# Fused chunk attention and Fourier mixing: how the first group's tables, weights and weight sums are spread over the engines

## The chip, the cores and the metric

The kernel runs on one core of a Trainium2 chip. A time is the device time of one execution in microseconds (us). A version is compared by the median of several executions; one further execution was recorded by the hardware profiler, and everything that is read from a trace is about that one. Instructions are issued by TensorE (PE), VectorE (DVE), ScalarE (ACT), GpSimd (POOL) and SyncE (SP). Each runs its own list in the order in which the program gives it. DMAs are issued from SP, ACT or POOL and wait in that engine's list until what they need is there.

## The reference

Two blocks follow each other. Shapes: batch 8, 8 heads, 576 tokens, head size 64, so 512 features; the MLP is 2048 wide.

```
# attention inside chunks of 64 tokens, per batch and head
scores = q_c @ k_c.T / 8                        # 64 x 64
attn   = exp(scores - max); attn /= sum(attn) + 1e-9
x      = attn @ v_c                             # heads side by side: (8, 576, 512)
# Fourier mixing and MLP
u   = x + real(fft(fft(x, over tokens), over features))
un  = (u - mean(u)) / sqrt(var(u) + 1e-6)       # over features
out = u + relu(un @ w_ch1) @ w_ch2              # 512x2048, 2048x512
```

The weights arrive as 64-bit floats and are turned into 32-bit ones on the chip; everything else is 32-bit. The Fourier transforms are products with tables of cosines and sines.

## The kernel before, in words

**Tiles and groups.** A tile is 128 tokens. Tiles 0 to 4 belong to batch 0: a "rest" tile (the middle chunk of batches 0 and 1), then LO(1), HI(1), LO(0), HI(0), pairs from the front and from the back of the sequence, which the transform folds onto each other (`fold`). Four tiles are a group for the MLP, group g being batch g's four tiles; the rests make a group at the end.

**Batch 0** is alone on the chip. `attention_early` (L507) runs the five tiles in a software pipeline: `att_T` transposes q and k on PE and copies them with ACT, `att_S` makes the scores, `softmax` uses DVE and ACT, `att_P` transposes back, `att_V` multiplies with v and normalizes on DVE. `shift_early` (L439) then moves single rows between tiles, since the fold needs token 0 apart; `fold` (L467) makes sums and differences. `fourier_early` (L686) multiplies them with the token table `tk` (L704 to L708), with the feature tables `cos_d`, `sin_d` (L734), adds the result to x, normalizes (`normed`, L770) and transposes (`turned`, L787) for the MLP. `keep_warm(n)` (L1098) gives PE n matmuls without a purpose of their own (each is two records in the trace).

**Tables.** `load_tables` (L221) loads the token table into `start` by eight DMAs and two rows into `first_rest` by two more. `turn_tables` (L245) copies it into `tk`, each run of 64 columns reversed, by four copies of 128x384 and two small ones.

**Weights.** `pieces` (L263) lists 32 pieces of 128x512, sixteen of each weight. `load_weight(i)` (L276) brings a piece into one of seven staging spaces; pieces from number 8 on have five of them, pieces from 26 on three. `round_weight(i)` (L284) starts piece i (two DVE and three ACT instructions: L295 to L299) and ends piece i-1 (three DVE instructions: L304 to L306), frees that piece's space and issues the next load. `round_next()` calls it for the next piece.

**The main loop** (L1144 to L1178) counts steps t. In a step `mlp(g)` gives PE one slice of the MLP: for group 0 steps 1 to 16 are the first product (four matmuls on one piece of the first weight), steps 17 to 32 the second one. Then `side(b)`, the next batch's attention and Fourier part, advances by as many steps as are due: batch 1 is spread over t = 3 to 25, batch 2 begins at t = 26. Its step 21 (at t = 22) and step 22 (t = 23) are the two halves of the token product L607, which ACT copies out of PSUM (L632 to L642); steps 23 to 25 (t = 24, 25, 25) are the feature products (L659) with additions and statistics. Then the step rounds weight pieces: none if the side step was a "heavy" one (a fold), else one, or two when t <= 4, t % 4 == 0 or t >= 18.

**Sums of the second weight.** From group 1 on the MLP uses a block scheme with seven products in place of eight, which needs sums of weight quarters. `keep2(i)`, i = 0 to 3 (L843), makes four sums of 128x512 (L854, POOL) and then stores seven parts to DRAM (L858); each sum and the store is a step of the generator `conv2`. The loop takes two of its steps per t, from t = 20 on (first five steps while the last pieces are rounded, then freely). `keep1` (L826) does the same for the first weight from t = 32 on.

**Normalization.** For group 1, and for the first tile of group 0, `normed` computes `shift = -mean * rstd` on DVE (L781) and lets ACT scale (L782).

**Order of the loads.** SP's list begins with q and k of tiles 0 to 4 (L205; k of tile 0 is on ACT), then weight 0 (L282), v of tiles 3 and 4 (L215, eight DMAs), the feature tables (L237, L238) and weights 1 to 6. POOL's list begins with v of tiles 0 to 2 and the ten DMAs of `load_tables`.

Of the kernel before, what the change touches and what calls it, by code (L numbers as in the profile page):

```python
# [10 lines left out]
ACTF = mybir.ActivationFunctionType  # L11
ALU = mybir.AluOpType
# [4 lines left out]
def kernel(  # L17
# [32 lines left out]
    nc = tc.nc  # L50
    B, H, S, D = q.shape
    DM = H * D
    DFF = w_ch1.shape[1]
    CH = 64
    NC = S // CH
    NM = 2
# [4 lines left out]
    KF = DFF // 128  # L61
    HM, HQ = DM // 2, DM // 4
    NQ = S // 2 + 1
    NS = (NQ + 3) // 4
    NL = 128 * NM
# [3 lines left out]
    scale = 1.0 / float(D) ** 0.5  # L69
# [44 lines left out]
    LO, HI, RE = "lo", "hi", "rest"  # L114
# [10 lines left out]
    at = {t: n for n, t in enumerate(tiles)}  # L125
# [15 lines left out]
    N_LATE, N_EARLY, N_LAST = 5, 8, 26  # L141
# [68 lines left out]
    def load_v(n):  # L210
        t = more_v[n - 3] if 3 <= n < first[1] else v_ring[n % 3]
        for i, (b, c) in enumerate(chunks(n)):
            for e in range(2):
                eng = nc.scalar if n == 0 and e else nc.gpsimd if n < 3 else nc.sync
                eng.dma_start(  # L215
                    out=t[e * CH:(e + 1) * CH, i, :, 0:D],
                    in_=v[b, e:H:2, c * CH:(c + 1) * CH, :].rearrange("j p d -> p j d"),
                )
        vs[n] = t

    def load_tables():  # L221

        t = start[:, 0:(NM + 1) * 2 * NQ].rearrange("p (i r f) -> p i r f", i=NM + 1, r=2)
        for c in range(2 * NM):
            (i, r0), (j, p0) = divmod(c * CH, 128), divmod((NC - 1 - c) * CH, 128)
            nc.gpsimd.dma_start(out=t[r0:r0 + CH, i], in_=seq_tab[p0:p0 + CH, j])
        for r0 in (0, CH):  # L230
            nc.gpsimd.dma_start(out=t[r0:r0 + 1, NM], in_=seq_tab[0:1, 0])
            nc.gpsimd.dma_start(out=t[r0 + 1:r0 + CH, NM], in_=seq_tab[1:CH, NM])
        for i in range(2):
            nc.gpsimd.dma_start(out=first_rest[32 + 32 * i:33 + 32 * i, 0:DM], in_=dim_tab[0:1, 1 + 2 * i, :])

    def load_dim_tables():
        nc.sync.dma_start(out=cos_d, in_=dim_tab[:, 0, :])  # L237
# [7 lines left out]
    def turn_tables():  # L245
        t = start[:, 0:(NM + 1) * 2 * NQ]
        a, b = tk.rearrange("p i r f -> p (i r) f"), t.rearrange("p (i f) -> p i f", f=NQ)
        for c in range(2 * NM):
            nc.gpsimd.tensor_copy(a[:, :, c * CH:(c + 1) * CH], b[:, :, (c + 1) * CH:c * CH:-1])
        nc.gpsimd.tensor_copy(a[:, :, NL:NL + 1], b[:, :, 0:1])  # L250
        nc.gpsimd.tensor_copy(a[:, :, NL + 1:NQ], b[:, :, NL + 1:NQ])

    def turn_dim_tables():

# [184 lines left out]
    def shift_early(i):  # L439

        lows = [xt(at[LO, 0, j])[:, 0:DM] for j in range(NM)]
        rest, kept = xt(rests[0])[0:1, 0:DM], first_rest[0:1, 0:DM]
        if i == 0:
            nc.gpsimd.tensor_copy(kept, lows[1][0:1])
            nc.gpsimd.tensor_copy(lows[1][0:1], lows[1][CH:CH + 1])
            nc.gpsimd.tensor_copy(lows[1][CH:CH + 1], rest)
        elif i == 1:
            nc.gpsimd.tensor_copy(rest, lows[0][0:1])
        else:
            nc.scalar.copy(lows[0][0:1], lows[0][CH:CH + 1])  # L450
            nc.scalar.copy(lows[0][CH:CH + 1], kept)

# [54 lines left out]
    def attention_early():  # L507

        lo, hi = first[0], first[1] - 1

        def ready(n):
            if n == at[LO, 0, 1]:
                shift_early(0)
            if n == at[HI, 0, 1]:
                fold(0, 1)
            if n == at[LO, 0, 0]:
                shift_early(1)
                fold(0, NM)
            if n == at[HI, 0, 0]:
                fold(0, 0)  # L520
            if n + 3 > hi:
                load_v(n + 3)

        att_T(lo)
        att_S(lo)
        for n in range(lo, hi + 1):
            if n < hi:
                att_T(n + 1)
            softmax(n)
            if n > lo:  # L530
                att_V(n - 1)
                ready(n - 1)
            if n == lo + 1:
                turn_tables()
            if n < hi:
                att_S(n + 1)
            if n in (lo, hi):
                keep_warm(1)
            att_P(n)
        shift_early(2)  # L540
        round_next()
        keep_warm(1)
        att_V(hi)
        ready(hi)
        round_next()

    def attention(b):
# [222 lines left out]
    def normed(g, s):  # L770
        if s >= len(groups[g]):
            return
        n = groups[g][s]
        if (g, s) == (0, 3):
            un = one_p.tile([128, NJ, 128], FP32, tag="pT", name="un").rearrange("p j t -> p (j t)")
        else:
            un = three_p.tile([128, DM], FP32, tag="o", name="un")
        mean, rstd = sts.pop(n)
        if g == 1 or (g, s) == (0, 0):
            shift_ = sm_p.tile([128, 1], FP32, tag="shift", name="shift")  # L780
            nc.vector.tensor_scalar(shift_, mean, rstd, -1.0, ALU.mult, ALU.mult)  # L781
            nc.scalar.activation(out=un, in_=natural(n), func=ACTF.Identity, scale=rstd, bias=shift_)  # L782
        else:
            nc.vector.tensor_scalar(un, natural(n), mean, rstd, ALU.subtract, ALU.mult)  # L784
        uns[g, s] = un
# [57 lines left out]
    def keep2(i):  # L843

        m = 2 * i
        b11, b12 = w2[:, m:m + 2, 0:HM], w2[:, m:m + 2, HM:DM]
        b21, b22 = w2[:, HF + m:HF + m + 2, 0:HM], w2[:, HF + m:HF + m + 2, HM:DM]
        to = xall[:, 2 * G:2 * G + 4, 0:DM] if i % 2 else yall
        o1, o2, o3, o4 = (to[:, j].rearrange("p (m e) -> p m e", m=2) for j in range(4))
        for out_, in0, in1, op in (  # L850
            (o1, b12, b11, ALU.subtract), (o2, b22, o1, ALU.subtract),
            (o3, b22, b12, ALU.subtract), (o4, b21, o2, ALU.subtract),
        ):
            nc.gpsimd.tensor_tensor(out=out_, in0=in0, in1=in1, op=op)  # L854
            yield
        to = s2.rearrange("o p (m e) -> o p m e", m=HF)
        for o, a in enumerate((b11, o2, o1, o3, b21, b22, o4)):
            nc.sync.dma_start(out=to[o, :, m:m + 2], in_=a)  # L858
        yield
# [13 lines left out]
    lo, hi = slice(0, 256), slice(256, 512)  # L873
# [199 lines left out]
    with tc.manual_schedule():  # L1073
# [9 lines left out]
        for n in range(first[1]):  # L1083
            load(n)
            if n < 3:
                load_v(n)
        load_tables()
        load_weight(0)
        load_v(3)
        load_v(4)  # L1090
        load_dim_tables()
        for i in range(1, len(spaces)):
            load_weight(i)
        n_w = 0
# [3 lines left out]
        def keep_warm(times):  # L1098

            for _ in range(times):  # L1100
                nc.tensor.matmul(out=idle[:, 0:NQ], lhsT=warm[:, 0:128], rhs=warm[:, 0:NQ], start=True, stop=True)

        def round_next():
            nonlocal n_w
            if n_w <= len(pieces):
                round_weight(n_w)
                n_w += 1
# [33 lines left out]
        n_conv = 0  # L1141
        conv2, conv1 = chain(conv2), chain(conv1)
        t = 0
        for g in range(NG):  # L1144
            for _ in mlp(g):
                t += 1
                heavy = False
                if cur < len(sides):
                    t0 = 2 if cur == 0 else ready_at[cur - 1]
                    t1 = ready_at[cur]  # L1150
                    due = min(sizes[cur], (t - t0) * sizes[cur] // (t1 - t0))
                    while done < due:
                        heavy = next(sides[cur], None) or heavy
                        done += 1
                    if t >= t1:
                        for _ in sides[cur]:
                            pass
                        cur, done = cur + 1, 0
                if not heavy:
                    round_next()  # L1160
                    if t <= 4 or t % 4 == 0 or t >= 18:
                        round_next()
                for _ in range(2):
                    if n_w > N_LAST + 2 and n_conv < 5 or n_w > len(pieces):
                        n_conv += 1
                        next(conv2, None)
                if t == begin[1] - 1:
                    for _ in conv2:
                        pass
                if begin[1] <= t < begin[1] + KF // 2:  # L1170
                    for _ in range(3):
                        next(conv1, None)
                if t == begin[1] + KF // 2:
                    for _ in range(NS2):
                        fetch(2)
                if t == begin[1] + KF:
                    for _ in range(NS1):
                        fetch(1)  # L1178
# [49 lines left out]
```

## Time and profile before

| what | us |
|---|---|
| median of 4 executions | 1126.31 |
| lowest and highest of them | 1124.85, 1128.12 |
| the profiled execution's own time | 1127.69 |
| its span on the core, first to last instruction | 1125.9 |
| PE busy in the span | 1092.0 |
| DVE, ACT, POOL busy | 570.3, 294.5, 309.0 |
| PE's first matmul of the MLP (L889) | starts at 50.99 |

The page of a profile has the busy time of every engine, the span in 40 slices with the clock that PE was granted, the DMA queues, the chain of work that ended last, and the costliest groups of instructions. A line of the timeline has a start and a duration in us, the engine, the line of the kernel, the operation, what it writes and reads, the shape, how many instructions are merged, and in brackets how long the engine was idle before it and what ended that. "PE z L607 <- ACT zr L635" says that PE's instruction of line 607, writing z, waited for ACT's of line 635. The view of stretches gives the busy time of each engine in a stretch, then PE's granted clock (1.00 is full), the busy share of the DMA engines and GB/s.

### The profile page before, as it was taken

The numbers are of one execution on the slowest core, as the hardware profiler recorded it, in microseconds if no ns is written. First come the engines' busy times: TensorE is split into PE (matmuls) and PEld (weight loads), VectorE is DVE, ScalarE is ACT, GpSimd is POOL, SyncE is SP. The second block draws the span as 40 slices with busy tenths as digits, with TensorE's granted clock in tenths as the row PEclk, the third lists the DMA queues.
The fourth block names the chain that finished last, engine by engine and source line by source line (L and its number), as shares of the span: only waits on it lengthen the run. The fifth ranks groups of instructions, "written<-read, shape, count | busy, mean of one in ns | idle before, by whom it ended". The sixth has DMA issues, their size and how long they took to land. (4 is left out here: it accounts for less than half of the span.)

```text
span 1125.9 us, 18754 instructions
## 1 busy us (share of the span) xinstructions
PE 1092.0 (97%) x7036; PEld 846.1 (75%) x7036; DVE 570.3 (51%) x1194; ACT 294.5 (26%) x710; POOL 309.0 (27%) x436
## 2 busy tenths in 40 slices
PE   7999989999999999999999999899999999999998
PEld 5644445446887888778888888788888888888887
DVE  4899975332555355563545355645455434423521
ACT  4688443221112311222122211222132102201210
POOL 6300137326403340053105130154015400130140
PEclk9999989999999999999999999999999999999999
DMA  9767555678475636872567356753654346546332
GB/s 192 224 179 187 153 194 164 182 246 277 163 218 154 177 120 208 235 202 85 173 197 201 125 171 196 218 159 116 203 194 118 113 139 204 141 146 197 91 113 75
DMA packets 147915, 192.73 MB, mean 171 GB/s; under 512 B 66261, under 2 KB 104153, under 8 KB 140657
## 3 DMA queue, kind: packets, MB, share of 16 engines
q1 hardware_dynamic: 145296, 189.57, 56.1%
q0 software_dynamic: 928, 1.57, 0.6%
q8 instruction: 56, 0.92, 0.3%
q10 hardware_dynamic: 1600, 0.39, 0.2%
q14 instruction: 35, 0.28, 0.1%
HBM read 167.22 MB, written 24.12 MB: 170 GB/s over the span
## 5 line engine op out<-in xcount | busy, mean ns | idle before, releaser
L879 POOL TENSOR_TENSOR h<-h 128x256 f32<-128x256 f32 x64 | 55.4, 871 | 414.0 <-PE pb L973 303.3
L1020 PE MATMUL pa<-wb,h 128*128 128x256 f32 x512 | 116.1, 381 | 0.0
L1020 PE MATMUL pb<-wb,h 128*128 128x256 f32 x512 | 115.0, 381 | 0.0
L973 PE MATMUL pb<-unT,wa 128*128 128x256 f32 x448 | 106.6, 381 | 4.3 <-DVE wa L982 4.3
L973 PE MATMUL pb<-wa 128*128 128x256 f32 x448 | 107.3, 382 | 1.4 <-DMA wa<-s 1.4
L973 PE MATMUL pa<-unT,wa 128*128 128x256 f32 x448 | 107.8, 383 | 0.0
L1020 PEld LDWEIGHTS pa<-wb,h 128*128 128x128 f32 x512 | 95.8, 190 | 14.6 <-issue 1.6
L1020 PEld LDWEIGHTS pb<-wb,h 128*128 128x128 f32 x512 | 95.8, 190 | 12.9
L973 PEld LDWEIGHTS pb<-unT,wa 128*128 128x128 f32 x448 | 84.3, 190 | 18.5 <-DVE wa L982 7.0
L973 PEld LDWEIGHTS pb<-wa 128*128 128x128 f32 x448 | 83.4, 190 | 14.7 <-DVE wa L980 1.9
L973 PEld LDWEIGHTS pa<-unT,wa 128*128 128x128 f32 x448 | 83.2, 190 | 11.6
L988 ACT ACTIVATE h<-pa 128x256 f32<-128x256 f32 x56 | 21.5, 384 | 176.4 <-PE pa L973 143.2
L889 PE MATMUL up<-unT,wa 128*128 128x512 f32 x128 | 58.0, 599 | 2.4 <-ACT h L897 1.6
L980 DVE TENSOR_TENSOR wa<-pa,wa 128x256 f32<-128x256 f32 x56 | 23.8, 425 | 70.3 <-PE pa L973 70.3
L927 PE MATMUL dn<-wb,h 128*128 128x512 f32 x128 | 57.7, 599 | 1.4 <-ACT h L897 1.4
L1020 PE MATMUL pa<-wb,yall 128*128 128x256 f32 x256 | 58.2, 382 | 0.0
L973 PE MATMUL pa<-wa 128*128 128x256 f32 x224 | 54.0, 384 | 3.8 <-ACT wa L978 3.8
L906 PE MATMUL up<-unT,wa 128*128 128x512 f32 x128 | 57.5, 598 | 0.0
L1020 PE MATMUL pb<-wb,yall 128*128 128x256 f32 x256 | 57.1, 380 | 0.0
L1020 PE MATMUL pb<-wb 128*128 128x256 f32 x256 | 56.6, 379 | 0.0
L1020 PEld LDWEIGHTS pb<-wb 128*128 128x128 f32 x256 | 48.2, 190 | 6.3
L1020 PEld LDWEIGHTS pa<-wb,yall 128*128 128x128 f32 x256 | 47.7, 190 | 6.9 <-issue 0.5
(235 smaller groups left out, 1676.6 us busy)
## 6 DMA issues: line engine op xcount, KB each, us to landing
wb<-s SPq DMA_DIRECT2D x56, 1024.0 KB
wa<-s SPq DMA_DIRECT2D x196, 256.0 KB
xall<-in_moe_w_ch_dram SPq DMA_DIRECT2D x22, 512.0 KB
q<-in_q_dram SPq DMA_DIRECT2D x96, 112.0 KB
k<-in_k_dram SPq DMA_DIRECT2D x96, 112.0 KB
v<-in_v_dram SPq DMA_DIRECT2D x124, 64.0 KB
yall<-in_moe_w_ch_dram SPq DMA_DIRECT2D x10, 512.0 KB
s<-wb SPq DMA_DIRECT2D x20, 256.0 KB
```

Of the source, the lines that this page charges most:

```text
L879: nc.gpsimd.tensor_tensor(out=h1[:, m, hi], in0=h1[:, m, lo], in1=h1[:, m, hi], op=ALU.subtract)
L889: nc.tensor.matmul(out=up, lhsT=w1[:, kk, m * 128:(m + 1) * 128], rhs=unT[:, kk], start=(kk == 0), stop=(kk == KD - 1),)
L906: nc.tensor.matmul(out=up, lhsT=w1[:, kk, m * 128:(m + 1) * 128], rhs=unT[:, kk], start=(kk == 0), stop=(kk == KD - 1),)
L927: nc.tensor.matmul(out=dn, lhsT=h1[:, m, s * 128:(s + 1) * 128], rhs=w2[:, m, :], start=(m == 0), stop=(m == KF - 1),)
L973: nc.tensor.matmul(out=dst, lhsT=w[:, kk, r], rhs=rhs[o][:, kk], start=(o in (0, 2) and kk == 0), stop=(kk == 1), skip_group_check=True,)
L980: nc.vector.tensor_tensor(out=b, in0=dst, in1=a, op=ALU.add)
L988: nc.scalar.activation(out=h1[:, m, lo], in_=dst, func=ACTF.Relu)
L1020: nc.tensor.matmul(out=dst, lhsT=lhs[:, m], rhs=w[:, m], start=(o in (0, 2) and m == 0), stop=(m == HF - 1), skip_group_check=True,)
```

## The change

The ten DMAs of `load_tables` are issued by SP, no longer by POOL, and come behind q, k and v of all five tiles; weight 0 comes behind them. `turn_tables` runs on ACT, no longer on POOL, and is called at the end of `attention_early`, behind the last tile's fold and three `keep_warm` matmuls; before, it was called in the loop's second round. The row copy of `shift_early(1)` moves from POOL to ACT and is joined with the two ACT copies of `shift_early(2)`; fold(0, NM) follows it. The two `round_next()` of `attention_early` come after all that. In the main loop the rule for a second `round_next()` is written otherwise; the second weight's sums begin only when all pieces are rounded and t >= 23, three generator steps per t, and run on DVE. The shift of group 1's normalization is made by two ACT instructions.

```diff
@@ load_tables: all ten DMAs
-            nc.gpsimd.dma_start(out=t[r0:r0 + CH, i], in_=seq_tab[p0:p0 + CH, j])
+            nc.sync.dma_start(out=t[r0:r0 + CH, i], in_=seq_tab[p0:p0 + CH, j])
...
@@ turn_tables
-            nc.gpsimd.tensor_copy(a[:, :, c * CH:(c + 1) * CH], b[:, :, (c + 1) * CH:c * CH:-1])
-        nc.gpsimd.tensor_copy(a[:, :, NL:NL + 1], b[:, :, 0:1])
-        nc.gpsimd.tensor_copy(a[:, :, NL + 1:NQ], b[:, :, NL + 1:NQ])
+            nc.scalar.copy(a[:, :, c * CH:(c + 1) * CH], b[:, :, (c + 1) * CH:c * CH:-1])
+        nc.scalar.copy(a[:, :, NL:NL + 1], b[:, :, 0:1])
+        nc.scalar.copy(a[:, :, NL + 1:NQ], b[:, :, NL + 1:NQ])
@@ shift_early
-        elif i == 1:
-            nc.gpsimd.tensor_copy(rest, lows[0][0:1])
         else:
+            nc.scalar.copy(rest, lows[0][0:1])
             nc.scalar.copy(lows[0][0:1], lows[0][CH:CH + 1])
             nc.scalar.copy(lows[0][CH:CH + 1], kept)
@@ attention_early
-            if n == at[LO, 0, 0]:
-                shift_early(1)
-                fold(0, NM)
...
-            if n == lo + 1:
-                turn_tables()
...
-        shift_early(2)
-        round_next()
+        shift_early(1)
+        fold(0, NM)
         keep_warm(1)
         att_V(hi)
         ready(hi)
+        keep_warm(3)
+        turn_tables()
+        round_next()
         round_next()
@@ normed
-            nc.vector.tensor_scalar(shift_, mean, rstd, -1.0, ALU.mult, ALU.mult)
+            if g == 0:
+                nc.vector.tensor_scalar(shift_, mean, rstd, -1.0, ALU.mult, ALU.mult)
+            else:
+                nc.scalar.activation(out=shift_, in_=mean, func=ACTF.Copy, scale=-1.0)
+                nc.scalar.activation(out=shift_, in_=shift_, func=ACTF.Identity, scale=rstd)
@@ keep2
-            nc.gpsimd.tensor_tensor(out=out_, in0=in0, in1=in1, op=op)
+            nc.vector.tensor_tensor(out=out_, in0=in0, in1=in1, op=op)
@@ order of the loads
+        load_v(3)
+        load_v(4)
         load_tables()
         load_weight(0)
-        load_v(3)
-        load_v(4)
         load_dim_tables()
@@ main loop
-                    if t <= 4 or t % 4 == 0 or t >= 18:
+                    if t <= 4 or t < KF and t % 4 == 0 or t >= KF + 3:
                         round_next()
-                for _ in range(2):
-                    if n_w > N_LAST + 2 and n_conv < 5 or n_w > len(pieces):
-                        n_conv += 1
+
+                if n_w > len(pieces) and t >= KF + 7:
+                    for _ in range(3):
                         next(conv2, None)
```

## The prediction

> **What bounds the kernel now.** I read the page first.
>
> ```profile
> PE 1092.0 (97%) x7036; PEld 846.1 (75%) x7036; DVE 570.3 (51%) x1194; ACT 294.5 (26%) x710; POOL 309.0 (27%) x436
> PEclk9999989999999999999999999999999999999999
> ```
>
> PE is busy for 97% of the span, and no part of the change removes a matmul from it. So only PE's waits can be won or lost, about 34 us in all, and time in which it runs below full clock: one slice has an 8. Second view, PE's waits in order of size:
>
> ```profile
> PE z L607 <- ACT zr L635: 5.1, 1, 5.1
> ...
> PE pt L316 <- DMA start<-in_k_dram: 1.7, 1, 1.7
> ...
> PE z L704 <- DVE pm L496: 1.0, 1, 1.0
> ```
>
> These three lie where the change works: the first in the second product of group 0, the others in batch 0's lone start. Third view, PE's timeline around the largest:
>
> ```profile
> 144.28 0.76 PE L607 MATMUL z<-tk,pm_rest 64*128 64x289 f32 x4
> 144.97 3.70 PE L927 MATMUL dn<-wb,h 128*128 128x512 f32 x8
> 153.72 4.22 PE L607 MATMUL z<-tk,pm 128*128 128x289 f32 x8 [5.06 <-ACT zr L635]
> 157.88 1.33 PE L607 MATMUL z<-tk,pm_rest 64*128 64x289 f32 x4
> ```
>
> The first half of L607 is done at 145.0. The second needs the PSUM tiles that ACT must copy out, and starts 5.06 us late. Then its matmuls take 4.22 and 1.33 us, where the first half's same ones took 2.11 (at 142.24) and 0.76: the stretch 153 to 155 has a granted clock of 0.50. The wait costs 5.06, the slow clock 2.11 + 0.57 = 2.7. Shorter waits (1.7 at 17.6, 1.6 at 66.5) drew no such stretch.
>
> Why ACT came late, on ACT's and DVE's timelines:
>
> ```profile
> 152.50 0.72 ACT L299 ACTIVATE power<-power,top 128x512 uint32<-128x512 uint32 x1
> 153.13 0.35 ACT L632 COPY zf<-z 128x256 f32<-128x256 f32 x1
> ```
>
> ```profile
> 139.65 1.50 DVE L297 TENSOR_SCALAR power<-xall 128x512 uint32<-128x512 uint32 x1
> 141.07 1.75 DVE L304 SCALAR_TENSOR_TENSOR wb<-xall,wb 128x512 f32<-128x512 uint32 x1
> 142.75 1.75 DVE L305 SCALAR_TENSOR_TENSOR power<-xall,power 128x512 uint32<-128x512 uint32 x1
> ```
>
> ```profile
> 139.31 1.55 POOL L854 TENSOR_TENSOR yall<-wb,yall 128x512 f32<-128x512 f32 x1 [7.83 <-DVE wb L306]
> 140.83 1.45 POOL L854 TENSOR_TENSOR yall<-wb 128x512 f32<-128x512 f32 x1
> 142.24 1.72 POOL L854 TENSOR_TENSOR yall<-wb,yall 128x512 f32<-128x512 f32 x1
> ```
>
> The copy stands in ACT's list behind the rounding of piece 30, and that waits for DVE, which runs pieces back to back at 2.6 us each from 133.9 on. While POOL makes the second weight's sums, DVE's instructions take 1.50, 1.75 and 1.75 where their usual rows say 0.42, 0.69 and 0.69, and the sum L480 at 130.25 (beside POOL's first L854) takes 1.77 instead of 0.69: 1.08 + 1.08 + 1.06 + 1.06 = 4.3 us of DVE lag, handed on to ACT and to PE.
>
> **Part 1, sums off POOL until t = 23.** Counting the loop by hand, all pieces are rounded at t = 22 before and after (the heavy steps are 16 and 18, so the two rules for a second rounding pick the same steps; that edit does nothing). No sum then runs beside the rounding, and the 4.3 us go. Next late is the weight load: pieces from 26 on share three spaces, and from a freed space (end of L305, 144.50, 147.10) to the first use of the piece loaded there (148.01, 150.76) the rows show 3.5 and 3.7 us, while DVE at full speed is back after 0.6 + 2.6 = 3.2 or 3.3. That gives 0.2 to 0.4 of waiting on each of some three pieces, of which I take 0.7 in all. PE's wait falls from 5.06 to 5.06 - 4.28 + 0.7 = 1.5, in the size that kept the full clock. **Gain 3.6 + 2.7 = 6.3.** If the clock falls all the same, only 3.6.
>
> **Part 2, sums on DVE.** Sixteen sums; the nearest row is L306 (two SBUF inputs, 128x512, 0.69, one every 0.61): 9.8 us of DVE, in counts 3, 2, 3, 2, 2, 3, 1 for t = 23 to 29. DVE has gaps there, 4.82 before 165.66 and 2.23 before 170.43, which hide those of t = 23 and 24. The three of t = 25 stand behind the last statistics (178.7) and ahead of batch 2's first softmax, which DVE now starts at 178.62 without a gap. So 3 x 0.61 = 1.8 later come that softmax, ACT's exponent behind it (180.04) and, next in ACT's list, group 1's first normalized tile.
>
> ```profile
> 180.58 0.80 ACT L782 ACTIVATE un<-xall,shift,rstd 128x512 f32<-128x512 f32 x1
> ```
>
> PE transposes that tile at 181.95, a slack of 0.6. The shift on ACT adds two instructions in front (a chained pair of that size, L596 and L597, takes 0.5) and takes off DVE one of 0.2 that nothing waited for. PE so waits 1.8 + 0.5 - 0.6 = 1.7; with DVE's usual slip I take 1.85. The sums of t = 26 to 29 delay transposes and a softmax whose consumers come 5 us later or more (PE's P at 199.5 follows a softmax done at 189.0). The 28 stores of 256 KB move on SP from 150 to 195 into 169 to 195, ahead of some q and k loads of batch 2, by about 3 us; those tiles are needed one or two steps (3.6 each) later, so nothing. **Loss 1.85, bounds 0 and 4.**
>
> **Part 3, the start.** The chain of before: k of tile 3 lands late (PE waits 1.71 until 19.26), POOL's fold(0,1) runs to 30.3, then POOL's row copy (0.60), two ACT copies until 32.17, DVE's fold(0,0), PE's L704 at 34.84, L734 at 38.70. `tk` was ready at 22.1, off the path.
>
> In the DMA view of 12 to 18 us POOL's queue takes 50.7, 65.5 and 45.6% of the engines and moves 0.83 MB, while SP's queue moves 0.25, 0.23, 0.25 MB per 2 us; alone, at 18 to 20, it moves 0.41. Without the tables q and k are some 0.5 MB ahead, 2.4 us. So the 1.71 goes, and with the 0.3 of idleness at 20.8 tile 4's end comes 1.9 earlier: the last P copy at 27.0, three ACT copies of 0.65 until 29.0, DVE's fold(0,0) done at about 32.5.
>
> What is late next is `tk`.
>
> ```profile
> 15.89 2.75 SPq L205 DMA_DIRECT2D start<-in_k_dram  x2
> 18.69 1.33 SPq L282 DMA_DIRECT2D yall<-in_moe_w_ch_dram  x1
> 20.13 6.38 SPq L215 DMA_DIRECT2D more_v<-in_v_dram  x8
> 26.55 0.60 SPq L237 DMA_DIRECT2D start<-in_dim_tab_dram  x1
> 27.20 0.44 SPq L238 DMA_DIRECT2D start<-in_dim_tab_dram  x1
> ```
>
> SP is through with k at 16.3 instead of 18.7, with v at 22.7 (eight at 0.8), with the eight table DMAs (rows L238, L282, L237: 0.43 to 0.60, I take 0.45) at 26.3. Landed, by the feature tables' 3 us from issue to the end of their traffic, at about 28.5; the issue price of v's rows, 0.8, would make it 31.3. Turning on ACT: 0.53 per 128x512 copy from SBUF (L296 to L298) gives 4 x 0.4, and 0.5 for the two small ones, 2.1 in all; POOL's own 2.3 is the other end. `tk` is ready at 31.3. From there PE runs without a gap: 2.38 for the first table block, 1.73 keep_warm, 3.86 to L734, which starts at 39.3 instead of 38.7. **Loss 0.6, bounds -1 and +3.** Hidden beside it: weight 0 (landed at about 30.5) and its rounding (4 us of ACT, 31.3 to 37, ahead of ACT's copies at 38.6); POOL's fold(0,NM), done at about 33; the feature tables, needed from 36.8 on POOL.
>
> The Trainium skill ("DMA: Bandwidth & Descriptors", section "Issuing engines are not separate DMA queues") speaks against a part of this: DMAs of all issuers run on the same engines and interleave, so another issuer saves only issue time. By that alone the 1.7 at k would stay and the sum be about -1.9. The rows of 12 to 20 us agree that the engines are shared, and for that reason the order, not the issuer, should free k; no run here shows it yet.
>
> **Sum.** -6.3 + 1.85 + 0.6 = -3.8. Against the profiled execution: 1127.69 - 3.8 = 1123.9. That execution lies 1.4 above the median, and I see no cause in these parts for that, so against the median 1126.31 - 3.8 = **1122.5**. Own range of this case, with part 2 at 0 to 3 and part 3 at -1 to +1.5: 1118.5 to 1124.
>
> **Rivals.**
> 1. *DVE or the loads become the bound* (chance 0.21). If a load takes 4.1 from the freed space, as the third row does (149.98 to 154.06), four pieces wait 0.8 each, PE's wait stays near 4 and the clock still halves: gain 1.1, sum +1.4, 1127.7. If instead PE waits 4 for group 1's first tile: sum -1.7, 1124.6. For it: three spaces, DVE without gaps. Against: the 4.1 stood behind stores (SP from 150.38) that move away. I give it as 1126.
> 2. *Slower: the tables land late and PE cools* (0.16). PE has no work from 29.6 until `tk`. If the table DMAs cost 0.8 each and q and k do not come sooner, SP ends them at 25.1 + 6.4 = 31.5, they land at 34, `tk` is ready at 36.1: 4.8 later than forecast, and from a wait of about 3.5 on (148.67 to about 152.3 in the large wait) the clock halves; as that slow stretch lasted 7 us, 3.4 more. Sum +4.4, **1130.7**. It decides from `tk` at 33.2 on. Against it: the DMA views of 22 to 25 and 25 to 28 us have means of 197 and 76 GB/s only, so the tables find free engines.
> 3. *The stall was not POOL's doing*: DVE would keep its 1.75 us instructions from some other source. The rows speak against it, since they begin and end with POOL's; in rival 1's price.
>
> **Chances.** Forecast 0.63, rival 1 0.21, rival 2 0.16. 0.2% is 2.25 us, about what a measurement of this kernel can tell from no change. The forecast case counts as faster, rival 1 as the same, rival 2 as slower. For 8 in 10 the range takes in the forecast's own range and rival 1's two prices: 1118.5 to 1128.
>
> **What would show it.** L607's second half within 2 us of L927's end and at 2.1 us; no DVE L304 or L305 of 1.75; PE waiting up to 2 us on `un` at group 1's first L316; L316 not waiting for k; L704's first start near 31 with ACT's `tk` copies as releaser. Wrong if L704 starts after 33, if the clock halves anywhere, or if DVE waits for weights by more than 1 us in all at t = 19 to 22.

## The result, and the profile after

The changed kernel takes 1124.17 us (median of 40 executions, 1121.79 to 1129.30), the kernel before beside it 1127.41 (63 executions): a ratio of 0.9975, 95% interval 0.9970 to 0.9981, that is 2.8 us less (2.1 to 3.4); the two medians themselves are 3.2 apart, and a change in us is given by the ratio from here on. The profiled execution of the changed kernel has a span of 1122.1 and a time of its own of 1123.96.

Line numbers shift a little in the changed kernel: the token product L607 is L604 there, L704 is L701, L734 is L731, the sums L854 are L855, the copies L632 and L635 are L629 and L632, L480 is L479, the MLP's L927 is L928, and `normed` has its shift in L781 and L782. Page first, the rows of PE and of its clock:

```profile
PE 1091.9 (97%) x7042; PEld 846.2 (75%) x7042; DVE 572.5 (51%) x1206; ACT 299.0 (27%) x725; POOL 276.8 (25%) x403
PEclk9999999999999999999999999999999999999999
```

POOL lost 32 us of work, and the 8 among the clock's digits is gone. PE's waits (each line: what waited, for what, us in total, how often, longest):

```profile
PE z L701 <- POOL pm_rest L501: 2.7, 1, 2.7
PE pt L316 <- ACT un L783: 1.8, 1, 1.8
...
PE z L604 <- ACT zr L632: 0.9, 1, 0.9
...
PE pt L316 <- DMA start<-in_k_dram: 0.4, 1, 0.4
```

The wait of 5.1 in the MLP's stretch is 0.9, and that for k 0.4 where it was 1.7; waits of 2.7 and 1.8 are new. PE's timeline around the token product of batch 1:

```profile
147.32 3.70 PE L928 MATMUL dn<-wb,h 128*128 128x512 f32 x8
151.97 2.22 PE L604 MATMUL z<-tk,pm 128*128 128x289 f32 x8 [0.94 <-ACT zr L632]
154.11 0.76 PE L604 MATMUL z<-tk,pm_rest 64*128 64x289 f32 x4
```

The second half runs at full clock, 2.22 and 0.76 in place of 4.22 and 1.33. DVE's pieces ahead of it, with the one wait for a weight that lies among these rows:

```profile
141.42 0.69 DVE L304 SCALAR_TENSOR_TENSOR wb<-xall,wb 128x512 f32<-128x512 uint32 x1
142.02 0.71 DVE L305 SCALAR_TENSOR_TENSOR power<-xall,power 128x512 uint32<-128x512 uint32 x1
...
146.28 0.43 DVE L295 TENSOR_SCALAR wb<-xall 128x512 uint32<-128x512 uint32 x1 [0.22 <-DMA xall<-in_moe_w_ch_dram]
```

No L304 or L305 of 1.75 is left. The new wait of 1.8, on DVE, ACT and PE in turn:

```profile
174.36 0.66 DVE L855 TENSOR_TENSOR xall<-wb,xall 128x512 f32<-128x512 f32 x1
174.93 0.68 DVE L855 TENSOR_TENSOR xall<-wb 128x512 f32<-128x512 f32 x1
175.54 0.69 DVE L855 TENSOR_TENSOR xall<-wb,xall 128x512 f32<-128x512 f32 x1
176.14 0.68 DVE L378 TENSOR_REDUCE mx<-sc 128x8 f32<-128x512 f32 x1
```

```profile
177.58 0.63 ACT L386 ACTIVATE ex<-ex 128x512 f32<-128x512 f32 x1 [2.57 <-DVE ex L380]
...
178.66 0.81 ACT L783 ACTIVATE un<-xall,shift,rstd 128x512 f32<-128x512 f32 x1
```

```profile
179.53 0.66 PE L316 MATMUL pt<-ident,un 128*128 128x128 f32 x4 [1.75 <-ACT un L783]
```

Three sums stand ahead of the softmax, its exponent on ACT is late, `un` stands behind the exponent, and PE behind `un`. Last, the start, on PE, on ACT, and by stretches (columns as told above, the engines being PE, PEld, DVE, ACT and POOL; the clock behind POOL's time is 1.00 in the first row and 0.50 in the others):

```profile
27.56 1.73 PE L1102 MATMUL idle<-warm 128*128 128x289 f32 x6
31.94 2.26 PE L701 MATMUL z<-tk,pm 128*128 128x289 f32 x4 [2.65 <-POOL pm_rest L501]
34.00 1.66 PE L701 MATMUL more_z<-tk,pm 128*128 128x289 f32 x4
```

```profile
29.72 1.76 ACT L249 COPY tk<-start 128x384 f32<-128x384 f32 x4 [1.13 <-DMA first_rest<-in_dim_tab_dram]
...
31.48 0.36 ACT L251 COPY tk<-start 128x192 f32<-128x192 f32 x1
```

```profile
28.00:30.00 2.00, 1.29 (x6) 0.67 (x4) 1.87 (x6) 0.87 (x2) 1.98 (x4) 1.00 0.67 146
...
33.00:34.00 1.00, 1.00 (x3) 0.68 (x2) 0.35 (x2) 0.00 (x0) 0.00 (x0) 0.50 0.96 348
34.00:35.00 1.00, 1.00 (x4) 0.71 (x3) 0.41 (x2) 0.89 (x2) 0.00 (x0) 0.50 1.03 399
```

ACT waits 1.13 for the table's DMAs (the view names a row DMA of `load_tables`; the copies read `start` alone) and ends its last copy at 31.84; PE starts at 31.94. The view names POOL, whose spans are rough; ACT is the releaser, since in each run below where this was read PE starts 0.1 behind ACT's L251. Then PE runs its first block at half clock: 3.65 for L701's first eight matmuls (31.94 until L704 at 35.59) where 2.11 is the same at full clock (31.77 to 33.88 in `e2_start_only` below).

For the experiments I cut each profiled execution at the same PE instructions: the first transposes, the start of tile 4's product with v (L407), the first feature product (L731), the MLP's first matmul, its first L928 behind the token product (step t = 24), group 1's first product. The stretch from L731 to the MLP takes 12.28 to 12.49 wherever it was cut and is left out.

| profiled execution | first transposes to tile 4's v | to L731 | MLP to t = 24 | t = 24 to group 1 | group 1 to the end | span |
|---|---|---|---|---|---|---|
| before | 21.75 | 9.64 | 108.74 | 40.22 | 925.95 | 1125.9 |
| after | 20.07 | 14.24 | 102.03 | 42.20 | 924.51 | 1122.1 |
| e1_sums_only | 24.27 | 9.59 | 102.10 | 42.50 | 925.56 | 1123.4 |
| e2_start_only | 19.89 | 11.59 | 108.94 | 40.22 | 923.49 | 1124.3 |
| e3_warm8 | 20.21 | 13.32 | 102.07 | 42.19 | 924.32 | 1122.6 |
| e4_tables_pool | 24.00 | 11.59 | 102.04 | 42.13 | 926.37 | 1125.5 |
| e9_v_pool | 23.70 | 11.60 | 101.96 | 42.19 | 926.13 | 1125.3 |
| e5_sums_pool_late | 20.06 | 14.31 | 108.73 | 40.38 | 927.68 | 1131.0 |
| e6_sums_dve_early | 20.15 | 13.83 | 103.21 | 41.72 | 929.04 | 1127.7 |
| e7_none_at_25 | 19.81 | 12.36 | 101.81 | 40.39 | 931.39 | 1126.1 |
| e10_mended | 20.04 | 13.70 | 102.14 | 41.22 | 928.70 | 1126.3 |
| e11_old_start | 22.44 | 9.59 | 102.22 | 41.16 | 930.83 | 1125.8 |
| e12_start_warm8 | 20.56 | 13.12 | 108.37 | 40.23 | 923.60 | 1126.2 |
| e13_six_at_23 | 19.98 | 13.74 | 101.96 | 40.39 | 926.04 | 1122.1 |

The two stretches of the MLP repeat within 0.6 for the same arrangement. The start and the long end vary by 1 to 3 us between executions of programs that are equal there, so a difference of that size in them needs timed runs. Part of that is the clock. It is at half for 3.41 us in the first column of e1, e4 and e9, in the second of after, e5 and e6, and in the last of e5, e6, e10, e11 and e13, and for 6.83 us in the last of e7 and in the MLP's of before, e2, e5 and e12; the last section tells what decides it.

### The profile page after: what moved, and what is told of

It is laid out like the page before. It is cut to its first block, busy times and chain, and to the rows that moved or that the text cites. A ratio compares the mean times of both kernels' runs of the same rounds, so it can differ in the third digit from the quotient of the medians.

```text
span 1122.1 us, 18759 instructions
## 1 busy us (share of the span) xinstructions
PE 1091.9 (97%) x7042; PEld 846.2 (75%) x7042; DVE 572.5 (51%) x1206; ACT 299.0 (27%) x725; POOL 276.8 (25%) x403
## 5 line engine op out<-in xcount | busy, mean ns | idle before, releaser
L928 PE MATMUL dn<-wb,h 128*128 128x512 f32 x128 | 57.7, 599 | 1.3 <-ACT h L898 1.3
```

What stands on the lines that cost most here:

```text
L928: nc.tensor.matmul(out=dn, lhsT=h1[:, m, s * 128:(s + 1) * 128], rhs=w2[:, m, :], start=(m == 0), stop=(m == KF - 1),)
```

## The experiments

**The two halves of the change alone.** First the kernel before with only the sums' part (KF is 16, so the sums begin at t = 23):

```diff
-                for _ in range(2):
-                    if n_w > N_LAST + 2 and n_conv < 5 or n_w > len(pieces):
-                        n_conv += 1
+                if n_w > len(pieces) and t >= KF + 7:
+                    for _ in range(3):
                         next(conv2, None)
@@ keep2
-            nc.gpsimd.tensor_tensor(out=out_, in0=in0, in1=in1, op=op)
+            nc.vector.tensor_tensor(out=out_, in0=in0, in1=in1, op=op)
```

> The kernel before with the second weight's sums alone changed (on DVE, from t = 23, three steps per t); start and shift as before. My theory (the sums beside the rounding cost PE 6.7 us at L607, and the sums of t = 25 cost 1.2 to 1.8 at group 1's first transpose): L734 at 38.7 as before, the wait at L607's second half about 1 us at full clock, a wait of 1.3 to 1.5 on un, in all -5.2 us (0.45% faster). Rival (the wait at L607 comes from the later start of the roundings in the changed kernel, not from the sums): the wait stays at 4 to 5 and the time within 1 us of before.

Measured 1124.98 (11 executions), ratio 0.9980 (0.9969 to 0.9991), -2.2 us. The two stretches of the MLP are as expected: 102.10 (-6.6) and 42.50 (+2.3, the shift on DVE stands behind sums). The total is not: this profile's start took 2.5 more than that of before, though nothing in the start was edited. Of that, 1.2 are later k (waits of 1.10 and 1.68; measured from the first transposes, the second ends at 13.13 here and at 11.95 in before), and the other 1.3 come behind it, where the clock is 0.50 from 22.13 to 25.54.

Second, the changed kernel with sums, loop and shift put back as they were:

> The changed kernel with sums, loop and shift as before, so the start alone is changed. My theory (the start costs 2.4 us, by a wait for tk and a halved clock): L734 at 41.1, the wait at L607 near 5 with a halved clock as before, in all +2.4 us (0.2% slower). Rival (the new start pays by itself): as fast as before or faster. If sums and start simply add, this run and the sums alone together give the whole change.

Measured 1128.35 (11 executions), ratio 1.0012 (1.0001 to 1.0024): +1.4. The wait of 5.1 and the half clock behind it are back, so the start has no part in them. In this profile ACT turns the tables from 29.55 on without a wait, PE is idle for 1.55 ahead of L701, and the clock stays:

```profile
31.77 1.21 PE L701 MATMUL z<-tk,pm 128*128 128x289 f32 x4 [1.55 <-POOL pm_rest L501]
```

**The clock in the start.** The changed kernel with more filling behind tile 4:

```diff
-        keep_warm(3)
+        keep_warm(8)
         turn_tables()
```

> The changed kernel with eight keep_warm matmuls in place of three ahead of turn_tables, so that PE's idle time before L704 is filled. Theory A (1.5 to 1.7 of the start's 2.4 us is the halved clock after an idle of 2.65): L704 starts at the same 31.9, its first blocks take 2.4 as before the change, L734 at about 39.5, 1.5 us faster than the changed kernel. Theory B (the blocks are slow for another reason, such as traffic on the tables): they stay at 3.9 and the time stays.

Measured 1123.29 (5 executions), ratio 0.9964 (0.9952 to 0.9977). The tables land later here (ACT's L251 ends at 34.04), and still the clock holds:

```profile
34.14 1.21 PE L701 MATMUL z<-tk,pm 128*128 128x289 f32 x4 [0.84 <-POOL pm_rest L503]
```

So the half clock follows PE's idleness and not the DMA traffic, which is as dense here (engines busy for 0.96 to 1.01 of 34 to 37 us). The expected 1.5 us is not shown by this pair: L731 starts at 41.74 in this profile, no earlier than in the changed kernel, and the ratios, 1.2 us apart, have overlapping intervals. Later the same filling was put into the start alone:

> The start part alone (sums on POOL and at their old steps, shift on DVE) with keep_warm(8) ahead of the table's turning. The start part alone with keep_warm(3) was measured at +1.4 (0.1 to 2.7). Theory A (what was mis-sized in the start is the clock that halves after the wait): no halved clock at L701, ratio 0.999 to 1.000, that is 0 to -1. Rival (the start costs its 1.4 through later tables whatever the clock): ratio 1.001 to 1.002.

Measured 1126.49 (12 executions), ratio 0.9993 (0.9982 to 1.0004): full clock in the start, 2 us less than the start with keep_warm(3) (the two were measured at different times, each against its own runs of the kernel before). A new wait of 0.74 comes up at L731: ACT's rounding now ends late enough to delay the `zf` copies.

**Who issues what in the start.** The changed kernel with the table DMAs on POOL again:

```diff
@@ load_tables: all ten DMAs
-            nc.sync.dma_start(
+            nc.gpsimd.dma_start(
```

> The changed kernel with the ten table DMAs issued by POOL as before the change, everything else as changed. Theory A (the place in the queues frees k): PE waits 1.7 for tile 3's k again, the tables have landed by 20, tk waits only for ACT's row copies (free at about 30.5) and is ready at 32.6, L704 no earlier than with SP and the idle before it about 1.5, so full clock: L734 at 40.3 to 40.8. Theory B (the transfer is shared whoever issues, so only issue time is saved): no wait on k, tk at 30.7, L734 at 38.7, 2.4 us faster than the changed kernel.

Measured 1126.52 (12 executions), ratio 0.9997 (0.9984 to 1.0010). The wait for k is back:

```profile
20.52 0.63 PE L316 MATMUL pt<-ident,start 128*128 128x128 f32 x4 [2.92 <-DMA start<-in_k_dram]
...
35.07 1.21 PE L701 MATMUL z<-tk,pm 128*128 128x289 f32 x4 [1.54 <-POOL pm_rest L501]
```

ACT turns the tables without a wait, so the stretch to L731 falls to 11.59; the one ahead of it rises by 3.9: 3.1 more of waiting for k (0.65 and 2.92 against 0.43 in the changed kernel), and a clock of 0.50 from 22.07 to 25.48. To see whether it is the table or any traffic from POOL, v of tiles 3 and 4 was issued by POOL in their place, tables on SP (`first[1]` is 5, the number of batch 0's tiles):

```diff
@@ load_v
-                eng = nc.scalar if n == 0 and e else nc.gpsimd if n < 3 else nc.sync
+                eng = nc.scalar if n == 0 and e else nc.gpsimd if n < first[1] else nc.sync
```

> The changed kernel with v of tiles 3 and 4 issued by POOL, so SP issues the tables right behind k, 5.6 us sooner. If the tables' landing is what tk waits for: they land by 25, ACT starts to turn them when its row copies end (28.6), tk at 30.8, idle before L704 about 1.2 and full clock, from tile 4's last product to L734 11.6 instead of 14.2 or 13.3. Price: 0.5 MB on POOL's queue beside q and k, so the wait for tile 3's k may come back by up to 1 us.

One execution, 1127.2. The stretches are those of e4 (23.70 and 11.60), with 0.45 and 1.57 of waiting for k and a clock of 0.50 from 21.79 to 25.20: whatever POOL sent beside q and k delayed k. None of the places tried is free; the delay is paid at k or at `tk`.

**What slowed DVE.** The changed kernel with the sums on POOL, at their new steps:

```diff
-            nc.vector.tensor_tensor(out=out_, in0=in0, in1=in1, op=op)
+            nc.gpsimd.tensor_tensor(out=out_, in0=in0, in1=in1, op=op)
```

> The changed kernel with the second weight's sums on POOL again, but at their new time (from t = 23). Theory A (the time of the sums decides, the engine doesn't): from the MLP's first matmul to t = 24 102.0 us as in the changed kernel, where before took 108.7; DVE's L304 and L305 at 0.69 throughout t = 19 to 22; and the wait for un at group 1's first transpose falls below 1, so t = 24 to group 1's first product takes 40.2 to 41 instead of 42.2. Theory B (the engine decides): 108 and 42.

One execution, 1132.85. My expectation failed, and in a way that teaches something: the sums of t = 23 did not run at t = 23. The first ran at 133.37, beside DVE's sum L479, which takes 1.77 instead of 0.69, and the next three so:

```profile
142.45 1.27 POOL L855 TENSOR_TENSOR yall<-wb,yall 128x512 f32<-128x512 f32 x1 [7.81 <-DVE wb L306]
143.68 1.45 POOL L855 TENSOR_TENSOR yall<-wb 128x512 f32<-128x512 f32 x1
145.08 1.46 POOL L855 TENSOR_TENSOR yall<-wb,yall 128x512 f32<-128x512 f32 x1
```

```profile
142.52 1.48 DVE L295 TENSOR_SCALAR wb<-xall 128x512 uint32<-128x512 uint32 x1 [0.21 <-DMA xall<-in_moe_w_ch_dram]
143.92 1.49 DVE L297 TENSOR_SCALAR power<-xall 128x512 uint32<-128x512 uint32 x1
145.33 1.76 DVE L304 SCALAR_TENSOR_TENSOR wb<-xall,wb 128x512 f32<-128x512 uint32 x1
147.01 0.68 DVE L305 SCALAR_TENSOR_TENSOR power<-xall,power 128x512 uint32<-128x512 uint32 x1
```

POOL's list has nothing in front of them, so they start as soon as their inputs are rounded (142.45), some 14 us before DVE reaches its sums of t = 23 in the changed kernel. Beside them DVE's instructions take 1.48, 1.49 and 1.76 in place of 0.43, 0.42 and 0.68, 3.2 us of lag and with L479 4.3, as in before; the wait at L604 is 5.12 with half clock, 4.2 more than in the changed kernel. These four sums (three of t = 23 and the first of t = 24) suffice for the whole stall. The counterpart: sums on DVE at their old steps, beside the rounding.

```diff
-                if n_w > len(pieces) and t >= KF + 7:
-                    for _ in range(3):
+                for _ in range(2):
+                    if n_w > N_LAST + 2 and n_conv < 5 or n_w > len(pieces):
+                        n_conv += 1
                         next(conv2, None)
```

> The changed kernel with the sums on DVE but in the old loop, two steps per t from t = 20. If what hurt was DVE and POOL side by side on the same memory port, DVE now carries about 3 sums of 0.6 more before L607's second half in place of 4.3 us of slowed instructions: wait at L607 some 2.5 to 3, from the MLP's first matmul to t = 24 104 us. If the sums themselves hurt, wherever they run, 108 as before.

One execution, 1129.48. The wait at L604 is 1.93 at full clock and the stretch 103.21, 1.2 above the changed kernel and 5.5 below before, though DVE does the early sums itself:

```profile
153.51 2.21 PE L604 MATMUL z<-tk,pm 128*128 128x289 f32 x8 [1.93 <-ACT zr L632]
```

So of the 6.7 that the sums' part gains here, 5.5 come from the engine and 1.2 from the later step; the later step alone, on POOL, gains nothing.

**The three sums of t = 25.** The changed kernel without them (they run one step later, as do all behind them):

```diff
-                if n_w > len(pieces) and t >= KF + 7:
+                if n_w > len(pieces) and t >= KF + 7 and t != KF + 9:
```

> The changed kernel without the three sums at t = 25 (they follow later). Theory A (they stand ahead of batch 2's first softmax and so of group 1's first normalized tile): PE's wait for un falls from 1.75 to 0 to 0.5, t = 24 to group 1's first product from 42.2 to 40.2 to 40.7. Rival (the two ACT instructions of the shift are the larger part): the wait stays above 1.2.

One execution, 1127.9. The wait for `un` is gone and the stretch is 40.39, but a wait of 5.3 ahead of an L407 at 251, and half clock from 249.33 to 256.16, swallowed the gain. I took that for an event of this execution, and combined the repairs:

```diff
@@ attention_early
-        keep_warm(3)
+        keep_warm(8)
@@ normed
-            if g == 0:
-                nc.vector.tensor_scalar(shift_, mean, rstd, -1.0, ALU.mult, ALU.mult)
-            else:
-                nc.scalar.activation(out=shift_, in_=mean, func=ACTF.Copy, scale=-1.0)
-                nc.scalar.activation(out=shift_, in_=shift_, func=ACTF.Identity, scale=rstd)
+            nc.vector.tensor_scalar(shift_, mean, rstd, -1.0, ALU.mult, ALU.mult)
@@ main loop
-                if n_w > len(pieces) and t >= KF + 7:
+                if n_w > len(pieces) and t >= KF + 7 and t != KF + 9:
```

> The changed kernel with three repairs: no sums of the second weight at t = 25 (they run one step later), the shift of group 1's normalization on DVE again in one instruction, and keep_warm(8) in place of keep_warm(3) ahead of the table's turning. Theory A (the sums' part is worth 6.7 in the MLP's stretch, and what the change gives back is the delay behind the three sums of t = 25, 1.8, and the slow clock in the token product, 1.3): no wait of PE for un, from t = 24 to group 1's first product 40.3 as before, from t = 24's start no halved clock, L731 near 40.2, and a time some 2.5 to 3 below the changed kernel, ratio to the kernel before 0.994 to 0.996. Rival (the stretches gained there are lost again later, for example because sums and stores move into batch 2's loads and the next group's start): the stretch from group 1's first product to the end is 2 or more longer than the changed kernel's 924.5 and the ratio stays at 0.9975.

Measured 1128.36 (11 executions), ratio 1.0009 (0.9998 to 1.0020): the rival. And the same steps with the old start (the kernel before with the sums' part, none at t = 25):

> The kernel before with the sums' part alone, and none of them at t = 25: start, tables, row copies and shift as before. Theory A: the MLP's stretch 102.0 (108.7 before), from t = 24 to group 1's first product 40.3, no wait for un; the start as before, from first transposes to tile 4's last product between 21.7 and 24.3 as it was in the executions with POOL's loads beside q and k, 9.6 from there to L731's counterpart; time 4 to 6.5 below before by the stages, ratio 0.9945 to 0.997, so at or within 1 of the mended kernel of this same job if the start part is worth nothing. Rival (the changed start is a gain on the median, since the old one loses up to 2.5 to late k): this one is 1.5 or more above the mended kernel.

Measured 1127.38 (12 executions), ratio 1.0005 (0.9995 to 1.0015), where the sums' part with those of t = 25 had given 0.9980. So the wait at L407 belongs to the edit. In e10_mended, on PE, and on SP some 50 us earlier (in this run's kernel L855 is the store):

```profile
252.64 0.91 PE L407 MATMUL xp<-v,pT 64*64 64x65 f32 x32 [3.98 <-issue]
```

```profile
195.73 1.80 SPq L192 DMA_DIRECT2D k<-in_k_dram  x4
197.58 0.43 SPq L855 DMA_DIRECT2D s<-wb  x1
198.05 1.61 SPq L855 DMA_DIRECT2D s<-xall  x3
199.70 1.72 SPq L855 DMA_DIRECT2D s<-wb  x2
201.53 0.64 SPq L855 DMA_DIRECT2D s<-xall  x1
202.26 3.19 SPq L215 DMA_DIRECT2D v<-in_v_dram  x4
```

The seven stores of the last part of the second weight (256 KB each) now stand between k and v of a tile of batch 2, where in the changed kernel v follows k at once (197.87, and group 1's first product is at 197.59 there, at 197.60 here). SP is 4.4 later from there on and does not catch up. The stretches, first of e10_mended, then of the changed kernel:

```profile
165.00:180.00 15.00, 14.22 (x78) 7.44 (x77) 12.16 (x24) 3.64 (x12) 3.56 (x3) 1.00 0.05 18
...
235.00:250.00 15.00, 13.66 (x65) 6.00 (x63) 2.00 (x5) 3.50 (x6) 4.04 (x4) 1.00 1.01 316
```

```profile
165.00:180.00 15.00, 13.25 (x72) 6.74 (x71) 12.12 (x24) 3.64 (x12) 3.37 (x2) 1.00 0.39 133
...
235.00:250.00 15.00, 15.00 (x99) 7.04 (x98) 6.54 (x17) 3.50 (x6) 2.49 (x5) 1.00 0.78 225
```

Without sums at t = 25 the DMA engines idle from 165 to 180 (busy 0.05 where they were 0.39), and from 235 to 250 they are full (1.01 where they were 0.78). The v that PE needs at 248.7 is issued at 248.20 instead of 243.27. "issue" as a releaser only says that the profile holds no event; the DMA's issue time shows the cause. Besides, the shift on DVE stands behind three sums of t = 26 and PE waits 0.78 for `un`: the two ACT instructions of the change are worth that much.

That gives a version to try: sums early enough for their stores, and still not at t = 25. DVE is idle for 2.4 us behind the three sums of t = 23 in the changed kernel, so three more go there; the shift stays on ACT.

```diff
@@ attention_early
-        keep_warm(3)
+        keep_warm(8)
@@ main loop
                 if n_w > len(pieces) and t >= KF + 7:
-                    for _ in range(3):
+                    for _ in range({7: 6, 8: 3, 9: 0}.get(t - KF, 3)):
                         next(conv2, None)
```

> The changed kernel, with the generator's steps counted 6 at t = 23, 3 at t = 24, none at t = 25 and 3 from t = 26 on, so the same number is done by t = 25 as in the changed kernel and its store instructions reach SP no later; the shift stays on ACT; keep_warm(8) as in the mended kernel. DVE has 161.3 - 158.9 = 2.4 us of idleness behind the three sums of t = 23, and three more take 1.8 to 2.0. Theory C (with no sums at t = 25 and the rest one step later, the stores of the second weight come behind q and k of batch 2's first tiles, SP gets 3 to 5 us behind and PE waits 4.0 to 5.3 for a v load at 250): no wait for un, no wait ahead of L407 at 248 to 253, 102.0 in the MLP's stretch, 40.4 from t = 24 to group 1's first product, 924 to 925 behind it, and a time 2 to 3 below the changed kernel: ratio 0.994 to 0.9965. Rival (the wait for v comes from something else that goes with removing the wait for un, such as PE reaching batch 2 earlier while SP's loads stay where they are): PE waits 1 to 3 ahead of L407 near 248, the stretch behind group 1's first product is 926 or more, and the ratio stays at 0.9975.

Measured 1120.64 (6 executions, 1120.13 to 1123.86), ratio 0.9940 (0.9928 to 0.9953): 6.8 below before, 3.9 below the changed kernel by the ratios, the fastest of all (keep_warm(8) alone, e3, is at 0.9964). PE at the two places, with no wait at either:

```profile
178.00 0.66 PE L316 MATMUL pt<-ident,un 128*128 128x128 f32 x4
```

```profile
247.04 0.70 PE L407 MATMUL xp<-v,pT 64*64 64x65 f32 x32
```

The profiled execution is the slowest of the six; its stretches of the MLP are 101.96 and 40.39 as expected, its end 926.04 is over the 924 to 925 expected. The clock is at half there from 264.84 to 268.25, behind a wait of 1.90 at L604; in the changed kernel the wait at that place is 1.49, and the clock stays.

## Why the prediction was right, and where it failed

The forecast was 1122.5 and -3.8. The measured median is 1124.17 and the change -2.8 (2.1 to 3.4 less): faster, as forecast. The median lies 0.2 above the own range as recorded, 1118.5 to 1124, and inside the wider one. The recorded ends do not follow from their parts: 6.3 gained, with part 2 at 0 to 3 and part 3 at -1 to +1.5, gives 1119.0 to 1124.5 from 1126.31. The four executions that the forecast started from were also 1.1 below the later median of the kernel before, 1127.41.

**Part 1 (gain 6.3): right.** 102.03 in place of 108.74 is -6.7: 4.1 of the wait (5.06 to 0.94; forecast 1.5) and 2.6 of the clock (2.00 at the first eight matmuls, 0.57 at the next four). The mechanism is shown from both sides: POOL's sums bring it all back (e5), the same sums on DVE at the old steps bring 1.2 (e6). Rival 1 had bet on late weights; the waits for them in this stretch are 0.34, 0.22 and 0.66, in all 1.2 where the three spaces were given 0.7. That is over the 1 us that I had named as a sign of being wrong, but the third, which ends at 152.35, comes when L604 already runs, and only 0.56 lie ahead of it. Rival 3 falls with e5 and e6.

**Part 2 (loss 1.85): right.** The wait is 1.75, the stretch +1.98, and without the three sums of t = 25 it is back at 40.39 (e7, e13). What I had cost at nothing, the stores that move by some 3 us, is nothing only just: a shift of 4.4 (e10) makes PE wait 4.0, and the same steps in e7 and e11 make it wait 5.3 and 4.0, each time with half clock around it. I had named a cover of one or two steps of 3.6. In e10_mended PE starts 4.4 behind v's issue; in the profile of before v is issued at 245.34 for a use at 250.94, so the slack there was 1.2, and those were the rows to look at.

**Part 3 (loss 0.6): the failed step, a size.** In the two profiles L731 starts 2.4 later than L734 did, and timed alone the part costs 1.4 (0.1 to 2.7). Two terms of it were mis-sized. `tk` is ready at 31.84 in place of 31.3: SP issues the table's first four DMAs at 0.63 each, not 0.45, and ACT gets the last of them at 29.7 where they were to land at 28.5; the turning takes 2.12 as estimated. And the clock, which I had forecast to hold, halves for the first block: 3.88 from L701 to the filling behind it (31.94 to 35.82) instead of 2.38. PE starts 0.6 later than forecast, the block takes 1.5 more and what follows 0.3 less, so 39.3 + 1.8 is the 41.08 of the profile. Rival 2 had this mechanism, but tied it to a wait of 3.5, read from one stall, and to `tk` from 33.2 on; the wait was 2.65 and `tk` came before that. So my own sign that the forecast would be wrong, a halved clock anywhere, did come, at a price smaller than rival 2's, and not in every execution: in 19 of the 40 the mean clock is 0.999 or 1.000, which leaves no room for 3.41 us at half (they alone take 0.0015 off the mean). The median of these 19 is 1123.65, that of the other 21 is 1124.90.

The gain of part 3 was rightly seen: order frees k. The first stretch falls by 1.7, and with POOL's traffic back beside q and k it rises to 24.0 and 23.7 (e4, e9), part of which is half clock. The Trainium skill ("DMA: Bandwidth & Descriptors", section "Issuing engines are not separate DMA queues") says that DMAs of every issuer share the same engines; e9 agrees, since with v on POOL PE waits 2.0 for k, with the tables there 1.7 (before) and 3.6 (e4). The conclusion I drew from the page alone, that the wait for k would stay, does not hold: the change does not only swap the issuer, it puts the tables behind k.

**The sum.** The profiled pair differs by exactly -3.8, which is chance: -6.7 and +2.0 in the MLP, +2.9 from the first transposes to L731, and -2.0 in stretches to which I had given nothing, -0.5 ahead of the first transposes and -1.4 behind group 1. The timed -2.8 fits the first three (-1.8) with the start at its timed +1.4 (-3.3), and does not decide between them.

What stays open: why k lands at different times in equal starts (PE waits 1.71 for it in before, 2.78 in e1 and 2.48 in e11); that, and the half clock that followed it in e1 alone, make the starts of one and the same program differ by 2 us and more. It is also open whether the start part is worth anything at all. With the filling it is at -0.8 (-2.0 to +0.5), and e10 and e11, which differ in little else, are at 1.0009 and 1.0005.

## What to carry to other kernels

When an elementwise engine runs slow instructions, look for the other one's instructions that begin and end with them; moving work to the engine that seemed busier gained 6.7 us in its stretch here, 5.5 of them by the engine alone. Place moved work by two questions, what stands behind it on its own engine, and when its stores must be through: three sums one step later removed a wait of 1.8 and made one of 4 in a load 50 us on, and the same sums two steps earlier removed both. An engine without anything in front of an instruction runs it as soon as its inputs are there, so a later place in the program delays nothing by itself.

## What the runs showed of the hardware

The granted clock is 1.00 or 0.50 in these 14 traces, and it changes on a grid: within one execution the stretches at 0.50 begin whole multiples of 3.413 us apart (in e5 at 32.54, 155.42 and 271.47, 36 and 34 times that) and last 3.41 or 6.83 us. What decided was how long PE idled inside one window of that grid. Leaving out the program's end, 16 stretches at 0.50 follow a window at full clock, and in each such window PE idled for 1.90 us or more. In none of the some 4,500 windows that were followed by full clock did it idle for more than 1.75. Two windows and what follows each, in the changed kernel and in e7 (PE's busy time stands behind the length, the clock behind POOL's):

```profile
28.23:31.64 3.41, 1.06 (x5) 0.49 (x3) 3.25 (x9) 2.28 (x7) 3.19 (x7) 1.00 0.79 189
31.64:35.05 3.41, 3.11 (x7) 2.27 (x8) 1.56 (x5) 1.14 (x3) 0.74 (x2) 0.50 0.99 340
```

```profile
30.88:34.29 3.41, 1.67 (x7) 1.38 (x8) 3.19 (x9) 2.06 (x7) 2.31 (x5) 1.00 0.71 223
34.29:37.70 3.41, 3.41 (x22) 2.36 (x21) 0.97 (x3) 2.06 (x4) 2.39 (x7) 1.00 1.01 386
```

The gap of 2.65 in the changed kernel lies in its window with 2.35; that of 2.31 in e7 is cut by a grid line at 30.88, 1.74 lie behind it, and the clock stays. A gap of 1.90 inside one window (e13) was enough. The grid lies differently in each execution, so one and the same wait can cost its own length in one and 1.3 to 1.5 us more in the next (what 3.41 us at half cost in e1 and in the changed kernel). The Trainium skill ("TensorE: Matmul & The Clock Gate", part 1 on the clock gate) tells of a free-running window of some 3.4 us that watches PE's activity; the grid of 3.413 agrees with that, and a limit on the length of a gap alone does not fit these rows.

DVE beside POOL's sums of 128x512: 1.48 to 1.50 for one-input instructions that take 0.42, and 1.75 to 1.77 for two-input ones that take 0.69, about 1.07 more per instruction in either form. The sums themselves take POOL 1.26 to 1.77, DVE 0.65 to 0.69.
